# Places for raw float64 weights, the order of the first weight fetches, and a new written order in a float32 attention + gated-layer kernel

## The chip, the core and the metric

The kernel runs on one core of a Trainium2 chip. TensorE (PE in the profile; PEld is its weight load), VectorE (DVE), ScalarE (ACT), GpSimd (POOL) and SyncE (SP, which here issues every DMA) run side by side, each through its own instructions in program order, and wait for one another on semaphores. The metric is the device time of one launch in microseconds (us), less is better.

## What is computed

Band attention for 8 batches of 8 heads (512 local rows of width 64, window 32, and 32 global rows per batch), followed by a gated layer over all 8 x 544 = 4352 rows of width 512:

```python
out_g = sm(scale * q_g @ [k_g, k_l]^T) @ [v_g, v_l]
out_l = sm([scale * q_l @ k_g^T, banded scale * q_l @ k_l^T]) @ [v_g, v_l]
x = rows of [out_g, out_l], heads side by side         # 4352 x 512
a = x @ w1;  b = x @ w2                                # 512 x 1024 each
h = (a * b) @ w3                                       # 1024 x 1024
out = h @ w_out                                        # 1024 x 512
```

q, k and v are float32. The four weight matrices arrive as float64 (20 MB), so the kernel fetches their 64-bit words raw and makes float32 of them on the chip.

## The kernel before

**Stages.** The weights go through three stages. A *fetch* (`fetch`, L621) brings 512 raw 64-bit words per partition (512 KB) or, for the pieces called `w12s`, 256 words (256 KB). An *unpack* is a shift on DVE (step 0, L593), a scaled activation on ACT (step 2, L595) and a merge on DVE (step 3, L597). For w1 and w2 (together `w12`, eight column blocks m of 128, a hi and a lo tile each) two steps more split the float32 into hi (step 4, `hi_of`, L356) and lo (step 5, `lo_of`, L359, on DVE or POOL). w3 and w_out are not split: their product W34 = w3 @ w_out is formed first, in 64 matmuls `fold(t, j)` (L675): row block t of w3, inner block j; eight j make one t in a PSUM bank, and `fold_split` makes hi (`w34h`) and lo (`w34l`) of it.

The attention takes 32 pairs of heads m in turn: load k, q and v (`k2`, `q2`, `v`), spread the keys (`kx`), scores on PE (`sp`, L377), a masked minimum for each of 8 tiles on DVE (`mmax`), exponentials on ACT, normalize, transposes and moves, the values on PE (`av`, L431 to L442). A batch's global rows have `sg` (L473), `mg`, `eg`, `ng`, `tg`, and go through DRAM (`tgo`, `tgi`). `xh` and `xl` split the result into the hi and lo of x. The gated layer takes 17 blocks k of rows; per quarter of the columns it has `first(k, m, c)` (12 matmuls, L539 to L541; `begin` is its first 9 where the fourth pair comes late), a gate on ACT, DVE and POOL (`ga`, `gb`, `gh`, `gl`), and `second(k, m)` (6 matmuls, L571 to L573).

**Order.** Nothing is scheduled when the program is built: `PLAN` (L72 to L201) is a written list, in which "478S" says that step 478 runs on SP; the number counts the calls of `add`. `list_schedule` reads it out and only asserts that a step's dependencies stand before it. So each engine's instruction order is fixed by that list. `COST`, `RATE` and the due times served to make the list and have no part in the run.

**Where raw words lie.** A fetched piece needs a place until its last reader is through. Pieces of 512 KB use a ring of four: three buffers `raw` in a pool `early` and the tile of the global values of odd batches (`VG1`), which is not used yet (`RAW`, L66). From the fifth fetch on, each waits for the steps on the piece four before it. The pool `early` (with w_out's float32 and two w3 tiles `w3f`) is closed before the tiles of m = 4 to 7 are opened in the same memory (`open_early`, `close_early`, L602 to L614). This is why w1 and w2 come in two forms: m = 0 to 3 as 8 pieces of 512 KB through the ring (`w12`), m = 4 to 7 as 16 pieces of 256 KB through the three output buffers `o` (`w12s`, `MA = 4`).

**Order of the fetches.** `ORDER` (L61) takes w3 by t: half a row block (j = 0 to 3, or 4 to 7) per piece, and w_out by j. The first eight fetches in it are w3(0,0), wo 0, w3(1,0), wo 1, w3(2,0), wo 2, w3(3,0), wo 3; a fold (t, j) needs the half of t that holds j, and wo j.

**Idle products.** `IDLE` (L49) puts 11 matmuls of 256 columns on zeros (`idle_products`, L312) ahead of everything on PE.

Of the kernel before, what the change touches and what calls it, by code (L numbers as in the profile page):

```python
# [69 lines left out]
W3F = ("w3f", "w3f", "g", "as", "gh", "gl")  # L70

PLAN = """  # L72
    478S 0V 6S 10S 18S 12A 1V 19D 7D 480D 11D 8A 9D 2593V 481A 479S 20A 13D 520S 14S 246P 521S 16A 15D 21D 17D 522A
    482P 247P 22S 26S 34S 30S 24A 523A 23D 25D 256P 562S 27D 491D 524P 2V 28A 533D 535D 327S 257P 483D 29D 32A 38S 604S
    525D 248P 266P 485D 493D 267P 31D 35D 495D 487D 33D 489D 36A 276P 42S 537D 564A 40A 37D 539D 268P 494A 538A 527D
    529D 497D 39D 531D 488A 41D 43D 530A 46S 536A 50S 44A 277P 54S 606A 342P 343D 45D 258P 249P 3V 58S 349D 48A 47D 49D
    532A 344A 345D 51D 446S 55D 250P 52A 53D 496A 259P 56A 346D 486A 57D 59D 62S 260P 278P 484A 66S 534A 347S 269P 251P
    492A 70S 270P 261P 498A 271P 350A 60A 279P 63D 61D 490A 150S 5V 272P 64A 326S 351D 540A 68A 526A 65D 499D 352D 71D
    74S 280P 72A 281P 67D 73D 500D 69D 252P 501D 262P 502D 353S 78S 282P 273P 253P 76A 283P 348S 82S 274A 508A 275D
    509V 156S 528A 79D 565V 284D 607A 507D 80A 286P 504A 75D 285D 541D 84A 287P 354S 288P 86S 254D 505V 503V 77D 506A  # L80
    83D 263P 289P 290P 85D 563S 510A 81D 542D 255D 87D 511P 543D 296P 88A 566P 297P 152A 544D 89D 547D 151D 90S 575D
    577D 512A 94S 567D 548V 91D 579D 550A 513A 158A 92A 569D 581D 153D 157D 98S 102S 264A 571D 95D 291P 292P 546A 93D
    578A 570A 306P 549V 447S 298P 514D 293P 96A 568A 580A 97D 551A 582A 545S 573D 99D 552A 265D 515V 574A 108S 299P
    605S 576A 307P 114S 100A 159D 308P 103D 572A 101D 316P 104A 294A 553P 583D 110A 300P 105D 120S 608P 584D 301P 109D
    106A 111D 518A 516A 585D 107V 302P 303P 112A 113V 295D 116A 586D 617D 115D 162S 618A 609D 126S 117D 132S 317P 646S
    588S 587A 554A 121D 519V 619D 122A 118A 591S 611D 555A 309P 621D 123D 310P 318P 119D 590V 620A 623D 556D 613D 517V
    622A 124A 624A 125D 127D 128A 163D 593S 304A 129D 133D 558A 311P 614A 559V 134A 138S 610A 130A 305D 615D 135D 164A
    136A 319P 312P 131D 616A 320P 612A 144S 165D 589S 592S 321P 322P 140A 313P 448S 329S 137D 560A 594A 139D 625D 141D
    146A 323P 142A 687S 314A 145D 626D 147D 648A 595P 324A 647S 148A 315D 596A 143V 325D 649D 149D 557V 449S 597A 598D
    154A 600A 155D 160A 650P 601D 628D 4V 728S 627D 1803P 730A 769S 166A 161V 167V 630D 602A 1805P 659D 636A 632V 651D  # L90
    1807P 633A 631A 634A 661D 635D 168S 170A 629D 688S 169D 662A 637P 663D 171D 653D 561D 665D 1809P 172A 174S 180S
    731A 638A 173D 639A 655D 328S 657D 175D 186S 729S 599V 176A 640D 182A 642A 177D 178A 355P 181D 183D 643D 184A 1804P
    664A 1806P 179D 185V 1808P 188A 356D 1811A 187D 1810P 1817P 450S 192S 189D 190A 362D 357A 641V 191V 1812D 358D 198S
    1813A 359D 363A 1818P 1814V 193D 364D 1819P 1815P 1816P 689A 194A 204S 1821A 360S 200A 660A 195D 199D 196A 810S
    451S 201D 644A 666A 1820P 202A 197D 206A 658A 365D 603V 203D 1827P 210S 205D 652A 366S 207D 654A 208V 656A 667D
    209V 1822D 1828P 668D 1823A 669D 670D 1824V 1829P 211D 212A 1830P 1831A 216S 213D 217D 1825P 218A 673A 214A 215D
    219D 361S 220A 222S 1826P 1832D 674A 221D 690D 671A 678A 676D 367S 228S 234S 677A 223D 1837P 224A 225D 672V 1839P
    675D 226A 691P 227D 230A 1833V 1834V 229D 231D 232A 236A 240S 235D 242A 233D 237D 241D 238A 700D 243D 701A 1835P
    244A 239V 692D 1836P 702D 694D 704D 703A 705A 245D 706D 645V 696D 695A 698D 1838P 693A 699A 707A 697A 679D 708D
# [983 lines left out]
```

## Time and profile before

| | us |
|---|---|
| median of 3 runs | 761.32 (760.6 to 761.7) |
| the profiled execution, all of it | 760.83 |
| its span, first to last instruction | 759.1 |
| PE busy | 744.2 (98%) |
| DVE busy | 444.0 (58%) |
| ACT busy | 326.1 (43%) |
| POOL busy | 77.4 (10%) |

The granted clock of TensorE is 0.996 over the span; 1.00 is 2.4 GHz, 0.50 is 1.2 GHz. A row of a timeline is: start, duration, engine, line, operation, output<-input, count, and in brackets the idle time before it and what ended it. A fold shows as two matmul records. Records of one engine overlap: the next starts before the one before it has ended.

### The profile page before, as it was taken

The page shows a single profiled execution, that of the slowest core. Times are in us where ns is not written, and L with a number is a line of the kernel's source. Part 1 is how long each engine was busy: PE and PEld are TensorE (multiplying, and loading weights), DVE is VectorE, ACT ScalarE, POOL GpSimd, SP SyncE. Part 2 cuts the span into 40 slices and gives each one's busy share as a digit, 9 for nine tenths or more (in the row PEclk, how much of TensorE's full clock was granted, in tenths as well). Part 3 has the DMA queues.
Part 4 walks back from the last instruction along what each step waited for, and adds up shares of the span by engine and source line. Part 5 has one row for each costly group of instructions (what it writes and reads, how often), then busy time and mean ns, then how long its engine had stood idle before and what let it go on. Part 6 is the DMA issues. An engine that isn't in the chain of part 4 may idle for free.

```text
span 759.1 us, 22082 instructions
## 1 busy us (share of the span) xinstructions
PE 744.2 (98%) x9228; PEld 652.0 (86%) x9228; DVE 444.0 (58%) x1351; ACT 326.1 (43%) x1000; POOL 77.4 (10%) x145
## 2 busy tenths in 40 slices
PE   7999799999999999999999999999999999999998
PEld 5344588989999999889998999889989999999997
DVE  3889987685665655483558465755567464412121
ACT  3757875543643343353445234444444343312111
POOL 2012331322000000000001011000001010000000
PEclk9999999999999999999999999999999999999999
DMA  8897675025312311241113311331113010000000
GB/s 282 306 279 247 212 205 162 17 73 147 119 60 70 115 46 31 75 136 57 48 39 103 114 49 46 94 117 32 59 33 118 16 44 6 32 1 29 1 28 28
DMA packets 44411, 69.72 MB, mean 92 GB/s; under 512 B 8120, under 2 KB 18584, under 8 KB 44312
## 3 DMA queue, kind: packets, MB, share of 16 engines
q1 hardware_dynamic: 44312, 68.32, 28.8%
q8 instruction: 72, 1.18, 0.6%
q14 instruction: 27, 0.22, 0.1%
HBM read 53.74 MB, written 13.37 MB: 88 GB/s over the span
## 4 chain that ended last, share of the span: by engine, by line
PE 83%; DVE 2%; ACT 1%; DMA 1%; issue 0%; POOL 0%; SPq 0%; DVEq 0%; ACTq 0%; POOLq 0%
PE bp L539 8%; PE ap L539 8%; PE acc L571 8%; PE acc L573 8%; PE acc L572 8%; PE ap L540 8%; PE bp L541 8%; PE bp L540 8%; PE ap L541 8%; PE s L377 4%; PE av L431 3%; PE av L440 2%; PE av L436 2%; PE sg L473 1%; DMA raw_w12s<-in_w_t_dram 1%; ACT P L388 0%
## 5 line engine op out<-in xcount | busy, mean ns | idle before, releaser
L539 PE MATMUL ap<-x,w12h 128*128 128x256 f32 x544 | 153.0, 281 | 0.7 <-ACT as__1656 L545 0.7
L539 PE MATMUL bp<-x,w12h 128*128 128x256 f32 x544 | 152.8, 281 | 0.0
L540 PE MATMUL ap<-x,w12h 128*128 128x256 f32 x544 | 151.1, 278 | 0.5 <-DVE x L359 0.5
L541 PE MATMUL ap<-x,w12l 128*128 128x256 f32 x544 | 151.0, 278 | 0.0
L541 PE MATMUL bp<-x,w12l 128*128 128x256 f32 x544 | 150.7, 277 | 0.0
L540 PE MATMUL bp<-x,w12h 128*128 128x256 f32 x544 | 150.7, 277 | 0.0
L388 ACT ACTIVATE P<-P,small 128x128 f32<-128x128 f32 x256 | 101.0, 396 | 28.5 <-DVE small L382 28.0
L539 PEld LDWEIGHTS ap<-x,w12h 128*128 128x128 f32 x544 | 102.5, 188 | 4.6 <-issue 1.8
L539 PEld LDWEIGHTS bp<-x,w12h 128*128 128x128 f32 x544 | 102.1, 188 | 5.0 <-issue 3.0
L382 DVE CUSTOM_DVE_ANT_0 P<-s,cs 128x128 f32<-128x128 f32 x256 | 64.7, 285 | 68.0 <-PE s L377 68.0
L540 PEld LDWEIGHTS ap<-x,w12h 128*128 128x128 f32 x544 | 102.6, 189 | 2.1 <-DVE x L359 0.7
L540 PEld LDWEIGHTS bp<-x,w12h 128*128 128x128 f32 x544 | 102.3, 188 | 1.6
L541 PEld LDWEIGHTS ap<-x,w12l 128*128 128x128 f32 x544 | 102.6, 189 | 0.0
L541 PEld LDWEIGHTS bp<-x,w12l 128*128 128x128 f32 x544 | 102.3, 188 | 0.0
L675 PE MATMUL w<-wo,w3f 128*128 128x512 f32 x128 | 58.6, 607 | 4.9 <-DVE wo L597 4.9
L420 ACT COPY PT<-TT 32x256 f32<-32x256 f32 (+1 forms) x98 | 38.0, 387 | 36.1 <-DVE TT L403 18.5
L675 PEld LDWEIGHTS w<-wo,w3f 128*128 128x128 f32 x128 | 23.6, 192 | 34.8 <-issue 22.9
L356 ACT COPY u<-av 128x512 f32<-128x512 f32 (+1 forms) x58 | 22.6, 399 | 63.5 <-PE av L442 61.6
L388 ACT ACTIVATION_READ_ACCUMULATOR P<-P,small 128x1 f32 x256 | 48.2, 188 | 0.0
L377 PE MATMUL s<-KT,qp 64*32 64x128 f32 x2048 | 38.6, 283 | 2.4 <-ACT w12h L356 2.4
L403 DVE STREAM_TRANSPOSE TT<-P 128x1024 f32<-128x1024 f32 x32 | 39.6, 1237 | 0.6
L398 DVE TENSOR_TENSOR P<-P,sums 128x1024 f32<-128x1024 f32 x32 | 39.2, 1225 | 0.6
(766 smaller groups left out, 1303.9 us busy)
## 6 DMA issues: line engine op xcount, KB each, us to landing
raw_w<-in_w_t_dram SPq DMA_DIRECT2D x24, 512.0 KB, 5.3
kq<-in_kp_t_dram SPq DMA_DIRECT2D x32, 272.0 KB, 3.9
out_dram<-o_None SPq DMA_DIRECT2D x33, 256.0 KB, 2.3
qp<-in_q_t_dram SPq DMA_DIRECT2D x32, 256.0 KB, 3.0
vr<-in_v_t_dram SPq DMA_DIRECT2D x32, 256.0 KB, 3.1
gg<-tgs SPq DMA_DIRECT2D x16, 272.0 KB, 2.2
raw_wo<-in_wo_t_dram SPq DMA_DIRECT2D x8, 512.0 KB, 5.8
raw_w12s<-in_w_t_dram SPq DMA_DIRECT2D x16, 256.0 KB, 3.9
```

The costliest lines, as they stand in the source:

```text
L377: nc.tensor.matmul(st[32 * a : 32 * a + 32, x, 128 * e : 128 * e + 128], q[r, 128 * e + 32 * a : 128 * e + 32 * a + 32], k[r, o : o + 128] ...
L382: nc.vector.tensor_tensor_reduce(Ps[m % 2][:, x, e], T["s", m][:, x, 128 * e : 128 * e + 128], masks[e], -0.125, 3.0e38, ALU.add, ALU.min, ...
L388: nc.scalar.activation(p, p, AF.Exp, bias=T["mn", n][:, e : e + 1], scale=-1.0, accum_out=T["sm", m][:, x, e : e + 1])
L398: eng.tensor_mul(p, p, view(T.pop(("sm", m)), 0, [1, 8], [0, 128]))
L403: nc.vector.transpose(view(TT[:], 0, [32, 8], [256, 4], [1, 32]), view(P, 0, [128, 8], [32, 4], [1, 32]))
L539: nc.tensor.matmul(d, wh[:, k, c, :], x[:, 0, 0:w], start=(k == m % 2 == 0), stop=False, skip_group_check=True)
L540: nc.tensor.matmul(d, wh[:, k, c, :], x[:, 1, 0:w], start=False, stop=False, skip_group_check=True)
L541: nc.tensor.matmul(d, wl[:, k, c, :], x[:, 0, 0:w], start=False, stop=(k == 3), skip_group_check=True)
L571: nc.tensor.matmul(a, gh[:, m % 2, sl], wh[:, c], start=(m == 0), stop=False, **part)
L572: nc.tensor.matmul(a, gh[:, m % 2, sl], wl[:, c], start=False, stop=False, **part)
L573: nc.tensor.matmul(a, gl[:, m % 2, sl], wh[:, c], start=False, stop=(m in (5, 7)), **part)
L675: nc.tensor.matmul(T["w34", t], T["w3f", t, j // 4][:, j % 4], T["wo"][:, j], start=(j == 0), stop=(j == 7))
```

## The change

1. **Places.** The pool `early` is gone. The hi and lo tiles of w1 and w2 (16 places of 4 KB per partition: h0, l0, ... h7, l7) exist from the start, and a place holds something else until its weight is made: h4, l4, h5, l5 hold w_out in float32; l7 holds two w3 tiles; raw words lie in h6, l6, h7, `VG1` and h0 to l3, twelve places. The first 24 pieces go round these twelve, eight more (m = 0 to 3) round the first four, and m = 4 to 6 through h6, l6, h7 and l7.
2. **Larger pieces.** w1 and w2 of m = 0 to 6 come as 14 pieces of 512 KB; only m = 7 comes as 4 pieces of 256 KB.
3. **w3 by rows.** The first half of w3 (t = 0 to 3) is fetched by j: piece `w3j` j holds block j of four t, so it and wo j give four folds. In DRAM that is four runs of 1 KB per partition instead of one of 4 KB. t = 4 to 7 come as before.
4. **Order.** A new list `PLAN`: PE's order differs only in its first 151 entries of 557; from entry 152 (`second(2, 2)`, 198.6 us into the span before) to the end it is as before, and the last 1623 entries of the whole list are the same on every engine. Deciphered, PE begins with sp(0), sp(1), fold(2,0), (0,0), (1,0), (2,1), (0,1), (3,0), (1,1), (3,1), sg(0), the four folds of j = 2, of 3, of 4 and so on; before it began fold(0,0), sp(0), fold(0,1), (1,0), sp(1), (1,1), (0,2), (2,0). SP begins k2 0, wo 0, w3j 0, q2 0, k2 1, q2 1, w3j 1, wo 1, k2 2, wo 2, w3j 2, k2 3, qg 0, w3j 3, wo 3, and so on by j to wo 6; then `tgo(0)`, w3j 6, w3j 7, wo 7, `tgo(1)`; before it began k2 0, w3(0,0), wo 0, wo 1, q2 0, k2 1, w3(1,0), q2 1, w3(2,0).
5. **Idle products.** 13 instead of 11.

The diff, cut (the lists of `PLAN` are left out):

```diff
-IDLE = {None: ((0, 128, 256),) * 11}
+IDLE = {None: ((0, 128, 256),) * 13}
...
 ORDER = (
-    *[(k, a, 0) for a in range(4) for k in ("w3", "wo")], *[(k, a, e) for a in range(4) for k, a, e in (("w3", a, 1), ("wo", a + 4, 0))],
-    *[("w3", t, e) for t in range(4, 8) for e in range(2)], *[("w12", m, e) for m in range(MA) for e in range(2)],
+    *[(k, j, 0) for j in range(8) for k in ("w3j", "wo")],
+    *[("w3", t, e) for t in range(4, 8) for e in range(2)], *[("w12", m, e) for m in range(7) for e in range(2)],
 )
-RAW = ((0, "raw", 3), (0, "raw", 3), (0, "raw", 3), (1, "VG1", 1))
+RAW = ("h6", "l6", "h7", "v", *[f"{x}{m}" for m in range(MA) for x in "hl"])
+RAW = (*[RAW[n % 12] for n in range(24)], *[RAW[n % 4] for n in range(8)], "h6", "l6", "h7", "h6", "h7", "l7")
-W3F = ("w3f", "w3f", "g", "as", "gh", "gl")
+W3F = ("70", "71", "g", "as", "gh", "gl")
...
+    def at_place(name, shape, dtype, what):
+        return weights.tile(shape, dtype, tag=name, name=what)
+    def wo_of(j):
+        x = ("h4", "l4", "h5", "l5")[j // 2]
+        if ("wo", x) not in T:
+            T["wo", x] = at_place(x, [128, 2, 512], F32, f"wo{j // 2}")
+        return T["wo", x][:, j % 2]
+    def w12_of(m):
+        if m not in W12:
+            W12[m] = tuple(at_place(f"{e}{m}", [128, 4, 2, 128], F32R, f"w12{e}{m}") for e in "hl")
+        return W12[m]
...
-        nc.sync.dma_start(raw.rearrange("p a w -> p (a w)"), i(src))
+        if kind == "w3j":
+            nc.sync.dma_start(raw.rearrange("p (a b) w -> p a (b w)", a=4), i(w3_t[0:4, :, a].rearrange("a p b -> p a b")))
+        else:
+            nc.sync.dma_start(raw.rearrange("p a w -> p (a w)"), i(src))
...
+    def w3_of(t, j):
+        return ("w3j", j, 0) if t < 4 else ("w3", t, j // 4)
...
-        nc.tensor.matmul(T["w34", t], T["w3f", t, j // 4][:, j % 4], T["wo"][:, j], start=(j == 0), stop=(j == 7))
+        nc.tensor.matmul(T["w34", t], w3f_of(t, j), wo_of(j), start=(j == 0), stop=(j == 7))
...
     def made(m):
-        if m < MA:
+        if m < 7:
             return [("unit", "w12", m, e, 5) for e in range(2)]
...
-            free = [*[("w34l", j) for j in range(8)], *[("unit", *x, 5) for x in ORDER if x[0] == "w12"]] if small else []
+            free = [("fold", y, 4 * (a - 4) + z) for y in range(8) for z in range(4)] if a in (4, 5) else []
+            for x in "hl":
+                free += [z for y in rings.get(f"raw{x}{a}", ())[-1:] for z in tiles[y]]
...
-    SMALL = [("w12s", m, e) for m in range(MA, 8) for e in range(4)]
+    SMALL = [("w12s", 7, e) for e in range(4)]
```

## Rows read from the trace of the kernel before

**Rows 1.** The page: busy time of each engine, and GB/s in 40 slices.
```profile
PE 744.2 (98%) x9228; PEld 652.0 (86%) x9228; DVE 444.0 (58%) x1351; ACT 326.1 (43%) x1000; POOL 77.4 (10%) x145
...
GB/s 282 306 279 247 212 205 162 17 73 147 119 60 70 115 46 31 75 136 57 48 39 103 114 49 46 94 117 32 59 33 118 16 44 6 32 1 29 1 28 28
```
**Rows 2.** Waits of PE: who waited for whom; us in total, times, longest.
```profile
PE w L675 <- DVE wo L597: 4.9, 3, 3.3
PE s L377 <- ACT w12h L356: 2.4, 1, 2.4
PE av L431 <- DVE raw_w L593: 1.4, 1, 1.4
```
**Rows 3.** Timeline of PE, the first 75 us.
```profile
1.19 7.28 PE L318 MATMUL idle<-TT 128*128 128x256 f32 x22 [1.19 <-DVE TT L316]
11.73 1.22 PE L675 MATMUL w<-wo,w3f 128*128 128x512 f32 x2 [3.26 <-DVE wo L597]
...
17.29 1.16 PE L377 MATMUL s<-KT,qp 64*32 64x128 f32 x64
...
26.31 16.12 PE L675 MATMUL w<-wo,w3f 128*128 128x512 f32 x36
```
**Rows 4.** Stretches: length, busy of PE, PEld, DVE, ACT, POOL, clock, DMA share, GB/s.
```profile
0.00:5.00 5.00, 3.81 (x9) 3.09 (x10) 0.27 (x1) 1.28 (x1) 4.07 (x21) 1.00 0.57 168
5.00:10.00 5.00, 3.47 (x14) 2.62 (x13) 0.96 (x3) 2.28 (x5) 1.32 (x4) 1.00 1.01 361
10.00:15.00 5.00, 3.27 (x67) 2.04 (x68) 3.28 (x7) 1.21 (x2) 0.00 (x0) 0.76 0.80 265
15.00:20.00 5.00, 4.62 (x71) 2.08 (x72) 3.25 (x15) 1.88 (x4) 0.00 (x0) 0.90 0.99 360
...
50.00:60.00 10.00, 10.00 (x164) 5.49 (x163) 9.80 (x31) 6.97 (x19) 1.33 (x3) 1.00 0.86 280
...
80.00:90.00 10.00, 6.17 (x155) 4.42 (x154) 9.83 (x20) 7.94 (x20) 3.55 (x4) 0.89 0.54 186
90.00:100.00 10.00, 9.52 (x164) 8.43 (x163) 8.92 (x38) 8.04 (x24) 2.54 (x6) 0.94 0.72 211
```
**Rows 5.** Timeline of SP's DMA issues, the first 40 us.
```profile
4.48 0.61 SPq L323 DMA_DIRECT2D qp<-in_q_t_dram  x1
11.10 0.33 SPq L638 DMA_DIRECT2D raw_w<-in_w_t_dram  x1
```
**Rows 6.** Waits of SP's queue.
```profile
SPq L638 <- DVE w3f L597: 15.6, 9, 5.0
```
**Rows 7.** Timeline of DVE, 8 to 60 us.
```profile
15.48 0.43 DVE L593 TENSOR_SCALAR raw_w<-raw_w 128x512 int32<-128x512 int32 x1 [2.20 <-DMA raw_w<-in_w_t_dram]
...
35.29 0.43 DVE L593 TENSOR_SCALAR raw_w<-raw_w 128x512 int32<-128x512 int32 x1 [1.46 <-DMA raw_w<-in_w_t_dram]
```
**Rows 8.** Groups by line: count, busy us, mean ns, idle before; unpack and split on DVE.
```profile
L593 DVE TENSOR_SCALAR raw_w<-raw_w 128x512 int32<-128x512 int32 x24 | 12.7, 528 | 4.8 <-DMA raw_w<-in_w_t_dram 4.7
...
L597 DVE SCALAR_TENSOR_TENSOR raw_w12s<-raw_w12s 128x256 int32<-128x256 int32 x16 | 7.8, 489 | 1.0 <-ACT raw_w12s L595 0.3
...
L597 DVE SCALAR_TENSOR_TENSOR raw_w<-raw_w 128x512 int32<-128x512 int32 x8 | 6.6, 827 | 0.1
...
L593 DVE TENSOR_SCALAR raw_w12s<-raw_w12s 128x256 int32<-128x256 int32 x16 | 5.4, 340 | 2.0 <-DMA raw_w12s<-in_w_t_dram 1.9
L682 DVE TENSOR_TENSOR w34l<-w,w34h 128x512 fp32r<-128x512 f32 x8 | 5.4, 679 | 0.1
...
L359 DVE TENSOR_TENSOR w12l<-raw_w,w12h 128x512 fp32r<-128x512 f32 x5 | 3.4, 678 | 0.0
```
**Rows 9.** Stretches chosen for their DMAs; columns as in rows 4.
```profile
9.00:11.00 2.00, 0.00 (x0) 0.00 (x0) 1.97 (x6) 0.73 (x2) 0.00 (x0) 1.00 1.03 414
246.00:254.00 8.00, 8.00 (x112) 7.23 (x93) 6.71 (x28) 4.98 (x21) 0.87 (x2) 1.00 0.50 126
...
181.50:186.00 4.50, 4.50 (x156) 3.96 (x156) 0.72 (x6) 0.00 (x0) 0.00 (x0) 1.00 0.83 267
```

More of the change, by code (lines that the diff above doesn't have):

```diff
@@ L201 @@
+    2550P 2554S 2555A 2556S
 """.split()
@@ L637, in fetch @@
             src = w12_t[a, :, 2 * e : 2 * e + 2].rearrange("p a b c -> p (a b c)")
-        nc.sync.dma_start(raw.rearrange("p a w -> p (a w)"), i(src))
+        if kind == "w3j":
+            nc.sync.dma_start(raw.rearrange("p (a b) w -> p a (b w)", a=4), i(w3_t[0:4, :, a].rearrange("a p b -> p a b")))
+        else:
+            nc.sync.dma_start(raw.rearrange("p a w -> p (a w)"), i(src))
         T[kind, a, e] = raw
@@ L646, in unit @@
             if step > 3:
-                hi, lo = (w[:, n * e : n * e + n].rearrange("p a b c -> p (a b c)") for w in W12[a])
+                hi, lo = (w[:, n * e : n * e + n].rearrange("p a b c -> p (a b c)") for w in w12_of(a))
             if step < 4:
@@ L682, in fold_split @@
             nc.vector.tensor_sub(W34[t][1], T.pop(("w34", t)), f(W34[t][0]))
+    weights = ctx.enter_context(tc.tile_pool(name="w12", bufs=1))
     steps, after, emit, rings, tiles, late, held = [], {}, [], {}, {}, [], {}
@@ L937, in weight @@
         me = [("unit", *u, j) for j in range(6)]
-        tag = "o" if small else "raw" if ORDER.index(u) % 4 < 3 else "rawv"
-        take(tag, dict(o=NO, raw=3, rawv=1)[tag], ("raw", *u), ("fetch", *u))
+        at = "o" if small else "raw" + RAW[ORDER.index(u)]
+        take(at, NO if small else 1, ("raw", *u), ("fetch", *u))
+        if at == "rawl7":
+            late.append((("fetch", *u), [("fold", *x) for x in sorted({(t, j) for t in range(8) for j in range(8) if w3f_at(*w3_of(t, j))[0] == "7"})]))
         add(("fetch", *u), dma(390), t - 12.0, (), fetch, *u, nbytes=(262144 if small else 524288))
@@ L946, in weight @@
         read(me[3], ("raw", *u))
-        if kind == "w3":
-            tag = W3F[[x[1:] for x in ORDER if x[0] == "w3"].index((a, e)) % len(W3F)]
-            take(tag, W3F.count(tag), ("w3f", a, e), me[3])
+        if kind[:2] == "w3":
+            take(w3f_at(*u), 1, (u, "f"), me[3])
         if kind[:3] == "w12":
-            free = [*[("w34l", j) for j in range(8)], *[("unit", *x, 5) for x in ORDER if x[0] == "w12"]] if small else []
+            free = [("fold", y, 4 * (a - 4) + z) for y in range(8) for z in range(4)] if a in (4, 5) else []
+            for x in "hl":
+                free += [z for y in rings.get(f"raw{x}{a}", ())[-1:] for z in tiles[y]]
             add(me[4], hi(COST["w12h"][s], 256 if s else 512), t + 1.5, [me[3], *free], unit, *u, 4, eng=True)
@@ L958, in product @@
         due = {u: W0 + WD * n for n, u in enumerate(ORDER)}
-        due = [max(due["w3", t, j // 4], due["wo", j, 0]) + FD for j in range(8)]
+        due = [max(due[w3_of(t, j)], due["wo", j, 0]) + FD for j in range(8)]
         take(BANKS[t], 2 if BANKS[t] == "acc" else 1, ("w34", t), ("fold", t, 0))
         for j in range(8):
-            deps = [("unit", "w3", t, j // 4, 3), ("unit", "wo", j, 0, 3)] + [("fold", t, j - 1)] * (j > 0)
+            deps = [("unit", *w3_of(t, j), 3), ("unit", "wo", j, 0, 3)] + [("fold", t, j - 1)] * (j > 0)
             add(("fold", t, j), only("PE", COST["fold"]), due[j], deps, fold, t, j)
-            read(("fold", t, j), ("w34", t), ("w3f", t, j // 4))
+            read(("fold", t, j), ("w34", t), (w3_of(t, j), "f"))
         add(("w34h", t), hi_psum(COST["w34h"], 683), due[7] + 2, [("fold", t, 7)], fold_split, t, 0, eng=True)
@@ L1015, in band_attention_glu_kernel @@
             k = steps[n][0]
-            if k[0] == "unit" and k[1] == "w12s" and k[4] == 4 and "w12b" not in P:
-                close_early()
             if eng:
```

307 lines of the change are left out of this document (147 added, 160 removed).

## Prediction

> **What bounds the kernel now.** The page comes first: PE is busy for 744.2 of 759.1 us [rows 1]. Work on the other engines is worth something only where PE waits for it, so no change that leaves PE's work alone can gain more than the 14.9 us in which PE is idle and what it loses at the lower clock. The waits of PE say where the idle time lies: 4.9 us for float32 weights ahead of folds, 2.4 us ahead of a score product, 1.4 us ahead of a value product [rows 2]. That is 8.7 us; 1.2 us pass before the first idle product [rows 3], and the rest, some 5 us, is small waits and the end of the program, which the change does not touch. The timeline places the first wait: the idle products end at 8.47 us, and PE stands for 3.26 us until the first fold at 11.73 [rows 3]; two more waits ahead of folds make up the other 1.6 of the 4.9. The other two rows lie between 80 and 90 us, where PE is busy for 6.17 of 10 us [rows 4].
>
> The granted clock falls after both long waits. It averages 0.76 and 0.90 in the stretches from 10 to 20 us, and 0.89 and 0.94 from 80 to 100 us [rows 4]. With two levels, 1.2 and 2.4 GHz, 5 x 0.24 + 5 x 0.10 = 1.7 us are lost in the first place and 10 x 0.11 + 10 x 0.06 = 1.7 us in the second, less what of it fell into idle time.
>
> Why do the inputs come late? SP issues its eighth load at 4.48 us and its next at 11.10 [rows 5]: the ring of four is full, and over the run its fetches wait 15.6 us for w3 merges alone [rows 6]. DVE in turn stands idle for raw words that were asked for late (2.20, 1.46 us) [rows 7], and this backlog is worked off only by a DVE that is full from 50 to 90 us (9.80 and 9.83 of 10 in the first and last of four stretches) [rows 4]. So the 3.8 us of waits near 85 us are DVE's queue being behind, and it is behind because fetches were gated.
>
> **Places and order of fetches.** With twelve places the first twelve pieces are issued without any wait, and up to the 24th each needs only the piece twelve before it. This takes the gate off, not the bandwidth. What the front needs, up to the last fold of t = 0 to 3: 16 pieces of 0.524 MB, four `k2` of 0.279, two `q2` of 0.262, `qg` 0.066 and one `tgo` of 0.279, in all 10.4 MB. Before, the DMAs moved 282 GB/s in the first 19 us and 306 in the next 19 [rows 1]: 5.35 MB, then 5.05 / 0.306 = 16.5 us, so 10.4 MB by 35.5 us even with the gate.
>
> When does PE want it? The front of the new order is sp 0, sp 1, 32 folds and sg 0. A fold is 16.12 / 18 = 0.90 us and an sp 1.16 [rows 3], an sg about the same. The four folds of j = 7 come after 28 folds, two sp and one sg: 25.1 + 3.5 = 28.6 us of PE work. From a start at 9.4 (below) that is 38.0; two unpacks on DVE ahead of it, 2 x (0.53 + 0.68 us) for a shift and a merge (the merge taken as long as the w34l row, another DVE pass over 512 float32) [rows 8], put the last landing at 35.6. So supply and demand meet with nothing to spare: I count 0 to 4 us of new waits here and take 1.
>
> **w3 by rows.** The same 512 KB in runs of 1 KB. This form is not in the trace. The nearest rows: loads in runs of 4 KB, 414 GB/s at a share of 1.03, so 402 at full share; runs of about 2 KB, 267 / 0.83 = 322; a mix with runs of 512 bytes, 126 / 0.50 = 252 [rows 9]. Eight pieces are 4.19 MB: 10.4, 13.0 or 16.6 us. The price is 0 to 6.2 us of DMA time, I take 3, by the nearer 2 KB. Against it stands the gap that vanishes: DMAs ran at 0.57 and 0.80 of their share in 0 to 5 and 10 to 15 us [rows 4], and the second, one us at full share, is now filled. On the end of the front that leaves the 1 us already taken, with the bound widened to 5.
>
> The Trainium skill speaks against this part: "DMA: Bandwidth & Descriptors", section "Why small descriptors are slow (HBM only)", gives a fixed cost of about three cycles per packet beside one per 32 bytes. By that a run of 1 KB costs 35 / 32 against 131 / 128 for 4 KB, an estimate of 7% or 0.7 us over the eight pieces, and the sum would be some 0.5 us better than with the value I took. The mixed rows above fall off more steeply than that.
>
> **Fold order.** A pair of pieces gives four folds instead of 1, 1, 2, 2 and so on. PE starts on sp 0, which needs only k, q and two key copies; the second pair was asked for in the first microseconds. The waits ahead of folds go: gain 4.9, and 1.7 of clock. What is late next: the first fold needs the DVE steps of w3j 0 and wo 0, and one minimum of pair 0 stands between them, so DVE cannot pass before sp 0 has ended. From sp 0's end to wo 0's merge: that minimum (128 columns, taken as no longer than a shift of 512), a shift and a merge, 0.53 + 0.53 + 0.68 = 1.7 us [rows 8] against 1.16 of sp 1 [rows 3], a new gap of 0 to 0.6; I take 0.5.
>
> **DVE's queue.** Counting the list: ahead of sp 4, which ended the 2.4 us wait, DVE has 142 steps before and 120 after. The main differences are 4 large shifts, 5 large w12 merges, 3 lo's, 3 small shifts, 3 small merges and 4 w34l fewer: 4 x 0.53 + 5 x 0.83 + 3 x 0.68 + 3 x 0.34 + 3 x 0.49 + 4 x 0.68 = 13.5 us by [rows 8], some 12 as records overlap by up to 0.08 us. PE has the same work ahead of it but one fold. Ahead of the first `begin` DVE has 11 steps fewer, ahead of the first complete `first` 18. So DVE, which was 2 to 3 us too late, gets about 12 us of room at sp 4 and 5 to 7 behind it, of which PE's earlier arrival (some 6 us) takes half or more. The waits of 2.4 and 1.4 us and the second 1.7 us of clock go. Bound: 0 to 2 us of smaller waits may come in their place; none taken beyond those above.
>
> Larger pieces: 12 small pieces become 6 large ones, on DVE 12 x (0.34 + 0.49) against 6 x (0.53 + 0.83): 1.8 us less, of no worth by itself, and inside the count above.
>
> **Idle products.** Two more of 256 columns, at half a fold of 512: 2 x 0.45 = 0.9 us on PE, on the path, since sp 0 stands behind them. Its inputs, the first four loads, are 1.59 MB; 168 GB/s to 5 us and 361 after it [rows 4] gives 7.1 us and about a us to be seen. So they end at 9.4, sp 0 can run from about 8.5, and 0.9 us is the full price; if the loads came later it would be nothing.
>
> **After 200 us** nothing moves: the list is the same on every engine. A lead gained in front is kept to the end.
>
> **Sum**, against the profiled execution (759.1 of span, 1.7 around it): 4.9 + 3.8 + 1.7 + 1.7 = 12.1 off; 0.9 + 1.0 + 0.5 = 2.4 on: 9.7 us less, 751.1 for that execution. The median of the runs shown stands 0.5 above it: 751.6. With no new waits 750; with the bounds of supply (5) and of smaller waits (2) in full, less the 1.5 taken, 757.
>
> **Rivals.**
> *The front is bound by supply.* Runs of 1 KB at the mixed rate cost 6.2 us, and waits of that length drop the clock again (1.7 us as before): 751.6 + 4 + 1.7 = 757.3. For it: DMA share is at 0.99 and 1.01 in two of the first four stretches [rows 4]. Against it: the last small fetches of the front were issued late because of the gate.
> *The places do not come free as counted*, so the change does not do what it says: SP still stands ahead of fetches, since a fetch into h0 to l3 or the split of w12 into them waits for a reader far down the list, or `tgo(0)` in SP's queue holds w3j 6, w3j 7 and wo 7 up. Then the waits near 85 us stay, with their clock: 751.6 + 3.8 + 1.7 = 757.1. Against it: `tgo(0)` waits for `tg(0)`, which stands ahead of wo 4 in DVE's queue.
> *Slower.* The place is w3j; the mechanism is a cost per packet and not per byte. If a packet of 1 KB took as long as one of 4 KB, the eight pieces would take 4 x 10.4 = 41.6 us of the DMAs, 31 more, and every fold of t = 0 to 3 would wait for them: 751.6 + 31 - 1 - the 6 or so us that the rest catches up, near 775. It decides from 10 us of lost supply on, that is from 4.19 MB in over 20 us, under 205 GB/s. The row with 512-byte runs still has 252 at full share, which speaks against it.
>
> **How the numbers follow.** Forecast (749.5 to 755) 0.67; better than that 0.05; supply 0.12; places 0.10; slower 0.06. The predicted time is 751.6, the range 749 to 758, which leaves out the slower case and the far ends. About 0.2% (1.5 us) is what a measurement of this kernel can tell from no change. Faster by more: all but the slower case and a little of the supply and places cases, 0.90; within it 0.04; slower 0.06.
>
> **What would show it.** SP issues a fetch at least every two us up to 25 us, with no pause as from 4.48 to 11.10. sp 0 starts at 9.4, folds by 12, and the 32nd fold ends near 42 to 44. The clock stays at 1.00 from 10 to 20 and from 80 to 100 us. PE waits for nothing over 1.5 us, and `second(2, 2)` starts near 189 instead of 198.6. DVE is no longer full from 50 to 90 us. I am wrong if PE has waits over 2 us before 45 us that end on a merge of w3j 5 to 7 (supply), or on score products near 80 us (places).

## The result and the profile after

The changed kernel takes 753.3 us (median of four executions, 753.15 to 755.88) beside 760.96 for the kernel before on the same chip: a ratio of 0.9905, 95% interval 0.9888 to 0.9922, so 7.2 us less by the ratio. Run again beside other kernels (below) the ratio was 0.992 (0.990 to 0.9941). The forecast was 751.6, 9.7 us less than the median that was known then (761.32). The direction held, and the waits that were to go are gone. A quarter to somewhat over a third of the gain is missing, and the reason that the prediction leaned on most, the gate on the fetches, turns out to be the smaller part. The profiled execution is the longest of its four: 754.1 us of span and 1.8 around it, 5.0 us of span less than before.

The waits of PE, to be read against [rows 2]: who waited for whom, us in total, times, the longest.

```profile
PE av L431 <- ACT PT L420: 1.6, 3, 0.8
PE w L684 <- DVE w3f L597: 1.2, 2, 1.1
...
```

None of the three rows of before is left. In their place stand eleven short waits in the first 113 us, none over 1.1 us. Their places are in the timeline of PE (the rows with idle time in brackets, and sp(0) with sp(1)):

```profile
1.18 7.90 PE L318 MATMUL idle<-TT 128*128 128x256 f32 x26 [1.18 <-DVE TT L316]
9.01 2.35 PE L377 MATMUL s<-KT,qp 64*32 64x128 f32 x128
11.86 7.48 PE L684 MATMUL w<-wo,w3f 128*128 128x512 f32 x16 [0.49 <-DVE wo L597]
...
21.27 14.17 PE L684 MATMUL w<-wo,w3jf 128*128 128x512 f32 x32 [0.84 <-DVE w3jf L597]
...
49.96 1.15 PE L377 MATMUL s<-KT,qp 64*32 64x128 f32 x64 [0.54 <-DMA qp<-in_q_t_dram]
...
57.53 1.98 PE L684 MATMUL w<-wo,w3f 128*128 128x512 f32 x4 [1.08 <-DVE w3f L597]
59.69 1.12 PE L684 MATMUL w<-wo,w3f 128*128 128x512 f32 x2 [0.17 <-DVE w3f L597]
...
82.99 0.38 PE L431 MATMUL av<-PT,vr 64*64 64x96 f32 x2 [0.41 <-ACT PT L420]
...
83.77 0.96 PE L431 MATMUL av<-PT,vr 64*64 64x128 f32 x27 [0.41 <-ACT PT L420]
...
89.24 0.38 PE L539 MATMUL ap<-x,w12h 128*128 128x256 f32 x1 [0.25 <-ACT x L356]
90.59 0.38 PE L540 MATMUL ap<-x,w12h 128*128 128x256 f32 x1 [0.96 <-DVE x L359]
...
97.30 0.39 PE L539 MATMUL bp<-x,w12h 128*128 128x256 f32 x1 [0.20 <-DVE g__1210 L549]
...
112.11 1.11 PE L431 MATMUL av<-PT,vr 64*64 64x96 f32 x30 [0.82 <-ACT PT L420]
```

The idle products are followed at once by sp(0) and sp(1), and from the first fold at 11.86 to 47 us PE has one wait of 0.84 us. The stretches, columns as in [rows 4]:

```profile
10.00:15.00 5.00, 4.39 (x83) 2.17 (x72) 4.17 (x14) 1.56 (x3) 1.68 (x4) 1.00 1.05 387
15.00:20.00 5.00, 5.00 (x26) 1.77 (x25) 3.67 (x27) 3.41 (x11) 0.97 (x2) 1.00 1.08 377
...
60.00:70.00 10.00, 10.00 (x165) 5.63 (x164) 9.90 (x27) 9.57 (x23) 5.47 (x6) 1.00 0.84 316
...
80.00:90.00 10.00, 8.56 (x201) 6.11 (x201) 9.76 (x29) 8.60 (x21) 3.79 (x3) 1.00 0.54 186
90.00:100.00 10.00, 9.21 (x76) 9.01 (x77) 9.62 (x26) 8.70 (x26) 4.54 (x5) 1.00 0.61 195
```

The granted clock is 1.00 where it was 0.76, 0.90, 0.89 and 0.94 [rows 4]. DVE, however, is as full as it was. What the lead is worth is seen at `second(2, 2)`, from which on the order is the same in both kernels; it started at 198.6 us before. This row groups the products of one source line and tile (minimum, median and maximum in ns, first and last start):

```profile
L571 PE MATMUL acc<-w34h,gh__2632 x4: 388/388/390, 192.7 to 194.8; 128*128 128x512 f32 x4
```

So the lead is 5.9 us there, where 9.6 were forecast. It can be added up. All that was to go has gone: 4.9 + 3.8 + 1.7 + 1.7 = 12.1. With it went two small waits which the forecast had left standing, 0.48 us near 99 us and 0.74 at 129. The timeline of PE in the kernel before shows the second of them, and the score product sp(4) with the old wait of 2.4 us:

```profile
87.71 1.96 PE L377 MATMUL s<-KT,qp 64*32 64x128 f32 x64 [2.42 <-ACT w12h L356]
...
129.20 0.38 PE L539 MATMUL ap<-x,w12h 128*128 128x256 f32 x1 [0.74 <-ACT as__1656 L545]
```

Gone are 13.3 us, then. Come instead: the idle products 0.6 (7.90 beside 7.28 us [rows 3]), the gap ahead of the first fold 0.5, and new waits of 0.84 + 0.54 + 1.08 + 0.17 + 0.41 + 0.41 + 0.25 + 0.96 + 0.20 + 0.82 = 5.7. That is 13.3 - 6.8 = 6.5, beside the 5.9 measured. The clock explains part of the difference: the prediction took it at 1.7 us for each of the two places in full, although some of it fell into idle time. The forecast had 1.0 us for the new waits in place of 5.7. The experiments ask three things: which part of the change made the old waits go, what the parts that cost something cost, and what the new waits come from.

### The profile page after: what moved, and what is told of

It reads as the page before. It is cut to its first block, busy times and chain, and to the rows that moved or that the text cites. A ratio compares the mean times of both kernels' runs of the same rounds, so it can differ in the third digit from the quotient of the medians.

```text
span 754.1 us, 22008 instructions
## 1 busy us (share of the span) xinstructions
PE 742.1 (98%) x9232; PEld 650.6 (86%) x9232; DVE 438.8 (58%) x1332; ACT 326.6 (43%) x989; POOL 84.3 (11%) x153
## 4 chain that ended last, share of the span: by engine, by line
PE 81%; DVE 7%; DMA 5%; ACT 3%; issue 1%; SPq 1%; DVEq 0%; ACTq 0%
PE bp L539 8%; PE ap L539 8%; PE acc L573 8%; PE acc L571 8%; PE acc L572 8%; PE ap L540 8%; PE ap L541 8%; PE bp L540 8%; PE bp L541 8%; PE s L377 4%; PE av L431 4%; DMA raw_w<-in_w_t_dram 3%; PE av L440 2%; PE av L436 2%; DMA raw_wo<-in_wo_t_dram 1%
## 5 line engine op out<-in xcount | busy, mean ns | idle before, releaser
L684 PE MATMUL w<-wo,w3f 128*128 128x512 f32 x96 | 43.4, 600 | 1.8 <-DVE w3f L597 1.2
L431 PEld LDWEIGHTS av<-PT,vr 64*64 64x64 f32 x1024 | 28.1, 132 | 13.0 <-issue 8.4
L462 POOL TENSOR_TENSOR xg<-u 128x32 f32<-128x32 f32 x32 | 8.7, 272 | 267.7 <-ACT u L356 233.4
```

The costliest lines, as they stand in the source:

```text
L431: nc.tensor.matmul(av[c, y, 128 * k + 32 * s0 : 128 * k + 32 * s1], V[r, x, k], PT[r, s0:s1, x, k], start=(k == 0), stop=False, **go)
L684: nc.tensor.matmul(T["w34", t], w3f_of(t, j), wo_of(j), start=(j == 0), stop=(j == 7))
```

## Experiments

All but the first were timed in five rounds, and all beside the kernel before on the same chip. The chips differ by some 0.2%, so the ratio to the kernel before is what compares.

| kernel | median us | ratio to before | 95% |
|---|---|---|---|
| changed, first time | 753.3 | 0.9905 | 0.9888 to 0.9922 |
| changed, again | 755.64 | 0.992 | 0.990 to 0.9941 |
| four places, by rows | 758.06 | 0.9936 | 0.9915 to 0.9957 |
| twelve places, by t | 760.95 | 0.9993 | 0.998 to 1.0007 |
| four places, by t | 763.94 | 1.0031 | 1.0012 to 1.0051 |
| before with 13 idle products | 761.8 | 0.9998 | 0.9984 to 1.0012 |
| changed with 11 idle products | 753.63 | 0.9888 | 0.9864 to 0.9912 |
| changed, w3 in whole runs | 755.13 | 0.9907 | 0.9887 to 0.9927 |
| changed, SP's order | 752.95 | 0.9873 | 0.9852 to 0.9894 |
| changed, GpSimd apart | 754.4 | 0.9904 | 0.9884 to 0.9925 |
| all moves together | 750.38 | 0.985 | 0.983 to 0.9871 |
| the same, w3 in whole runs | 749.03 | 0.983 | 0.9811 to 0.9849 |
| the same, runs of 1 KB, DVE's order | 749.18 | 0.9831 | 0.981 to 0.9852 |

The changed kernel again, as the yardstick of the second batch:

> The changed kernel once more, beside the next three on the same chip. It sets what they are compared with. Expected: ratio 0.990 to 0.992 to the kernel before, as in its first measurement, with the same new waits ahead of folds, of the first value products of pair 3 and near 90 us.

It came out at 0.992 with the same new waits (1.05 us ahead of a fold near 57 us, 0.69 for a load of q, 0.97 near 90 us). Below, 0.9912 stands for the changed kernel, the mean of its two ratios.

### Which part took the old waits away

**Four places.** The order on each engine is that of the changed kernel; only eight of the first 16 pieces lie elsewhere.

```diff
-RAW = (*[RAW[n % 12] for n in range(24)], ...
+RAW = (*[RAW[n % (4 if n < 16 else 12)] for n in range(24)], ...
```

> The changed kernel with four places, not twelve, for the first 16 pieces of weights (the eight by rows of w3 and the eight of w_out); the order of the instructions on every engine is as it was. My theory: it was the ring of four that made the inputs of the folds late. SP again stands for several us after its eighth load or so, the folds of the first 45 us wait for 4 us or more in all, the granted clock falls below 1.00 after the longest of these waits, and the program is 4 to 8 us longer than the changed kernel: 757 to 761. Rival (the gain comes from the order by rows alone, which asks for less before the first four folds, and the places matter little): 753 to 755, with SP's pauses hidden behind folds.

SP's issues show the gate again, as in [rows 5]: it stands from 5.9 to 12.8 and from 16.2 to 23.0 us.

```profile
5.05 0.86 SPq L329 DMA_DIRECT2D kq<-in_kp_t_dram  x1
12.79 0.33 SPq L637 DMA_DIRECT2D raw_wo<-in_wo_t_dram  x1
...
15.91 0.33 SPq L637 DMA_DIRECT2D raw_wo<-in_wo_t_dram  x1
22.95 0.38 SPq L635 DMA_DIRECT2D raw_w3j<-in_w_t_dram  x1
```

Yet PE hardly felt it. Its waits for folds of this kernel:

```profile
PE w L684 <- DVE w3f L597: 2.9, 3, 1.7
...
PE w L684 <- DVE wo L597: 1.1, 2, 0.8
...
PE w L684 <- DVE w3jf L597: 0.8, 1, 0.8
```

That is 4.8 us beside 2.5 in the changed kernel, the granted clock stays at 1.00, and the time is 0.9936 against 0.9912: 1.8 us, with intervals that overlap, where my theory said 4 to 8. Neither theory as written holds in full. The gate is real, but by rows most of its wait falls beside folds that are there to be done.

**By t.** Twelve places, but the first half of w3 by t, and the 32 folds in the order of the kernel before, in the slots where the folds of t = 0 to 3 stood. (Two DVE steps of w3(3,0) had to stand ahead of a minimum of the global scores, or the order would have locked.)

```diff
 ORDER = (
-    *[(k, j, 0) for j in range(8) for k in ("w3j", "wo")],
+    *[(k, a, 0) for a in range(4) for k in ("w3", "wo")], *[(k, a, e) for a in range(4) for k, a, e in (("w3", a, 1), ("wo", a + 4, 0))],
...
-        return ("w3j", j, 0) if t < 4 else ("w3", t, j // 4)
+        return ("w3", t, j // 4)
```

> The changed kernel with twelve places as it is, but the first half of w3 fetched by t again, half a t in each piece, and the 32 folds of t = 0 to 3 in the order in which the kernel before had them, in the places of the list where the folds stood. My theory: both parts were needed for the front. By t the folds that a new pair of pieces allows are 1, 1, 2, 2 and not four, so PE runs out of folds before 20 us although the fetches are early: waits ahead of folds of 2 to 5 us in all before 40 us, and the program is 2 to 6 us longer than the changed kernel. Rival: the early fetches are all that matters; then the time stays within 1 us of the changed kernel's and the fetch by rows has no worth of its own.

The time is that of the kernel before, 6.2 us above the changed kernel by the ratios, just past the end of what I had expected. PE's timeline, two of its seven waits ahead of folds before 40 us, and the stretch from 10 to 15 us:

```profile
15.64 2.84 PE L684 MATMUL w<-wo,w3f 128*128 128x512 f32 x6 [1.80 <-DVE wo L597]
...
32.39 5.55 PE L684 MATMUL w<-wo,w3f 128*128 128x512 f32 x12 [2.24 <-DVE wo L597]
...
10.00:15.00 5.00, 3.34 (x130) 1.97 (x130) 4.34 (x16) 1.64 (x3) 1.50 (x4) 1.00 1.04 416
```

In all PE waits 8.3 us for w_out and w3 here, with every fetch issued early. By t, k pieces allow about k x k / 4 folds (1, 4, 9, 16 after 2, 4, 6, 8 pieces); by rows 2 k (4, 8, 12, 16). PE runs dry between pieces although the DMAs move over 400 GB/s from 10 to 20 us.

**Neither.** Both edits at once.

> Both parts of the front undone in the changed kernel: four places for the first 16 pieces, and the first half of w3 by t with the folds in the order of the kernel before. It fills the fourth corner beside twelve places by rows (the changed kernel), four places by rows (0.9936 of the kernel before) and twelve places by t (0.9993). My theory now: by t the folds are short of pairs even when every fetch is early, so the gate adds little there, 0 to 2 us: 761 to 763, about the kernel before, and what the rest of the change gains near 85 us is given back by a list that was not made for this front. Rival: places and rows are separate gains that add up; then it is 2 to 3 us slower than twelve places by t, 763 to 764, a ratio of 1.002 to 1.004.

The rival came true: 1.0031, 2.9 us above twelve places by t. So the two parts nearly add up: by rows instead of by t is worth 6.2 us with twelve places and 7.2 with four; twelve places instead of four 1.8 us by rows and 2.9 by t. The waits ahead of folds do not show what the places are worth by t: they add up to 8.3 us in the kernel with neither, too. In the profiled executions the clock differs. After a wait of 2.2 us near 32 us, twelve records of folds took 7.11 us in the kernel with neither and 5.55 (above) by t with twelve places. The stretch from 35 to 40 us (the clock is the third number from the right) has 0.80 with neither and 1.00 by t with twelve places:

```profile
32.96 7.11 PE L684 MATMUL w<-wo,w3f 128*128 128x512 f32 x12 [2.23 <-DVE wo L597]
...
35.00:40.00 5.00, 5.00 (x10) 1.92 (x8) 4.02 (x12) 2.03 (x5) 0.00 (x0) 0.80 0.97 365
```

```profile
35.00:40.00 5.00, 3.70 (x9) 1.44 (x8) 4.80 (x11) 3.07 (x8) 0.00 (x0) 1.00 0.72 270
```

These are single executions. Over all of them, the mean clock of the span is 0.993 to 0.998 with neither and 0.995 to 0.999 by t with twelve places (0.996 or less in eight of twelve), and 0.999 or 1.000 by rows, with four places as with twelve. So the clock tells rows from t and not twelve places from four; what makes up the 2.9 us is not settled.

One limit: the rest of the list was made for rows. By t in a list made for it need not be as bad: the kernel before, by t with four places in its own list, waits for folds for only 4.9 us [rows 2], where the kernel with neither waits for 8.3. So the 6 to 7 us are the price of t in this list. Another limit: the runs with four places give them to the first 16 pieces only.

### What the parts that cost something cost

**Idle products.** First the kernel before with 13 of them, `IDLE` alone changed.

> The kernel before with 13 idle products instead of 11; nothing else. It tells whether the two products have a part in the granted clock's staying up. My theory: PE still waits for the first merge, so the products end inside that wait and cost nothing; the wait gets about 0.6 us shorter, the granted clock still falls below 1.00 between 10 and 20 us, and the time is the same within 0.5 us. Rival: the shorter wait no longer takes the clock down; then it is 1.00 from 10 to 20 us and the program is 1 to 2 us shorter, and up to 1.7 us of the change's gain belong to the idle products and not to the fetches.

The time is the same (0.9998). The wait ahead of the first fold is 2.76 instead of 3.26 us, and the granted clock falls all the same (10 to 15 us, the column before the DMA share):

```profile
12.05 1.61 PE L675 MATMUL w<-wo,w3f 128*128 128x512 f32 x2 [2.76 <-DVE wo L597]
...
10.00:15.00 5.00, 2.95 (x58) 1.71 (x66) 3.58 (x8) 1.46 (x3) 0.00 (x0) 0.76 0.74 252
```

So the two products alone do not keep the clock up. Then the changed kernel with 11.

> The changed kernel with 11 idle products ahead of the first score product instead of 13; nothing else differs. My theory: the two products lie in time in which the inputs of the first score product are already there, so leaving them out lets it start about 0.6 us earlier (0.62 us is what the two cost by the two profiles, 0.9 us is what I had taken), and the program is 0.3 to 0.9 us shorter, near 752.7, with the granted clock still at 1.00 after 10 us. Rival: the first score product then waits for its loads, and the time is the same within 0.3 us. Second rival: the clock is held up by these two products; then it falls below 1.00 between 10 and 20 us and the program is 1 to 2 us longer.

The ratio is 0.9888 against 0.9912, 1.8 us better, with intervals that overlap. The clock stays at 1.00, so the second rival is out. That would be more than the products' own time. In the profiled execution the waits of 0.54, 1.08 and 0.17 us between 49 and 60 us are missing, too. Whether that follows from the earlier start is not settled: sp(0) started at 8.07 us here and at 8.44 in the second profile of the changed kernel, which had them. SP, however, was through the second group of loads of `tgi` (below) at 42.6 us here, and at 45.4 and 44.1 in the two profiles of the changed kernel.

**Runs of 1 KB.** A second copy of the half of w3 in DRAM, by rows in whole runs.

```diff
-            nc.sync.dma_start(raw.rearrange("p (a b) w -> p a (b w)", a=4), i(w3_t[0:4, :, a].rearrange("a p b -> p a b")))
+            nc.sync.dma_start(raw.rearrange("p a w -> p (a w)"), i(w3j_t[:, a]))
```

> The changed kernel, with a second copy of the first half of w3 in memory, laid out so that each piece by rows lies in whole runs of 4 KB instead of runs of 1 KB. Everything else is as it was. My theory in the prediction took 3 us of DMA time and 1 us of the end for the short runs. After the look at the changed kernel's profile, where the DMAs moved 370 to 400 GB/s at a full share while these pieces arrived, I expect no difference: 753.3 within 0.5 us, and the idle stretch of the DMAs near 25 us only begins up to 1 us earlier. Rival (the front is bound by supply, because of the short runs): the time falls by 1 us or more, and the waits ahead of folds before 60 us get shorter by as much.

No difference beyond the intervals: 0.9907. The DMAs do see one. Packets and the queue's share of 10 to 20 us, first of the changed kernel (again), then of this one:

```profile
DMA packets 2437, 3.81 MB, mean 381 GB/s; under 512 B 143, under 2 KB 1785, under 8 KB 2436
...
q1 hardware_dynamic: 2436, 3.79, 105.9%
```

```profile
DMA packets 1384, 4.11 MB, mean 411 GB/s; under 512 B 151, under 2 KB 279, under 8 KB 1383
...
q1 hardware_dynamic: 1383, 4.10, 102.7%
```

Whole runs go at 4.11 MB / 10.27 us = 400 GB/s at full share. In the first, some 1640 packets of 1 KB are 1.68 MB; the other 2.13 MB at 400 take 5.3 of the 10.6 us, which leaves 5.3 for the 1.68 MB: about 320 GB/s. By this estimate the eight pieces cost 13.1 instead of 10.5 us of the DMAs, 2.6 us. The profile of whole runs shows where these go: the DMAs are nearly idle at 24 to 28 us, in all for some 2 us more than in the changed kernel.

```profile
24.00:26.00 2.00, 1.90 (x5) 0.57 (x3) 1.72 (x4) 2.00 (x8) 0.00 (x0) 1.00 0.15 59
26.00:28.00 2.00, 1.94 (x5) 0.98 (x6) 1.93 (x8) 2.00 (x10) 0.00 (x0) 1.00 0.03 8
```

### What the new waits come from

**SP's order.** In the changed kernel the DMAs run dry while SP stands. The rows show its issues, and then two stretches:

```profile
16.19 1.15 SPq L637 DMA_DIRECT2D raw_wo<-in_wo_t_dram  x2
26.70 0.33 SPq L504 DMA_DIRECT2D gg<-tgs  x1
27.08 1.15 SPq L635 DMA_DIRECT2D raw_w3j<-in_w_t_dram  x2
...
40.38 4.50 SPq L510 DMA_DIRECT2D TGr<-gg  x4
```

```profile
26.00:28.00 2.00, 2.00 (x7) 0.79 (x5) 2.00 (x5) 2.00 (x7) 0.00 (x0) 1.00 0.25 85
...
42.00:44.00 2.00, 2.00 (x6) 0.90 (x5) 1.21 (x5) 1.98 (x8) 0.00 (x0) 1.00 0.38 80
```

`tgo(0)` (L504) holds SP for 9 us with three fetches behind it; `tgi` (L510) and its waits do the same near 40 us. The edit lets fetches pass.

```diff
+for w, x in (
+    ("54S", "311S"), ("62S", "311S"), ("66S", "311S"),   # w3j 6, w3j 7, wo 7 ahead of tgo(0)
+    ("70S", "317S"), ("78S", "317S"), ("74S", "317S"),   # three of w3 ahead of tgo(1)
+    ("86S", "318S"), ("102S", "318S"), ("527S", "290S"), # w3, w12 ahead of tgi(1); q2 2 ahead of vg
+):
+    PLAN.remove(w)
+    PLAN.insert(PLAN.index(x), w)
```

> The changed kernel with nine entries of SP's list moved: the last two pieces of w3 by rows and the last of w_out ahead of the first store of the summary scores (which waits for DVE), three pieces of w3 ahead of the second, two pieces ahead of its loads, and one load of q ahead of the loads of the values. My theory: the waits that are new in the changed kernel at 50 to 60 us (0.5 + 1.1 + 0.2 us) come from SP's queue, where fetches stand behind an instruction that waits, while the DMAs run dry from 24.5 to 27.5 and from 42 to 48 us. They then go, and the program is 1 to 1.8 us shorter, near 752. Rival: DVE's queue sets these waits and the fetches were early enough; then nothing changes within 0.4 us. Second rival: the fetches now delay the second half of the summary scores, whose reader, the first value product near 48 us, waits up to 3 us, and the program is 1 to 3 us longer.

0.9873, 3.0 us better, more than expected. The waits of 0.54, 1.08 and 0.17 us are gone, and the DMA share is 1.12 in both stretches above. Nothing but SP's list was touched, so letting fetches pass a waiting SP is enough to take them away. They come to 1.8 us; the rest of the 3.0 is within the intervals. That the run with 11 products lacked them too, with SP's list as it was, fits SP's being through with `tgi` earlier there, but was not tested by itself.

**GpSimd beside VectorE.** In that run a shift on DVE took 1.60 us and delayed a fold by 1.05; near 87 us a step `xl` took 1.31. POOL's rows of the same kernel say what it did then (DVE first, then POOL):

```profile
13.81 1.60 DVE L600 TENSOR_SCALAR raw_wo<-raw_wo 128x512 int32<-128x512 int32 x1
...
87.21 1.31 DVE L366 TENSOR_TENSOR x<-u,x 128x256 fp32r<-128x256 f32 x1 [0.21 <-ACT x L363]
```

```profile
13.29 0.95 POOL L314 MEMSET VG<- 128x1024 f32 x1
14.18 0.96 POOL L307 MEMSET PT<- 128x1024 f32 x1
...
86.95 1.29 POOL L366 TENSOR_TENSOR w12l<-raw_w,w12h 128x512 fp32r<-128x512 f32 x1 [1.63 <-ACT w12h L363]
```

The shift ends at 15.41, 0.27 us behind the end of the second clear; without company it takes 0.43. The merge ahead of it, from 13.21 us on, kept its usual 0.69 us beside the first clear. The moves for these two steps in a kernel of their own:

```diff
+    ("3V", "487V"), ("2V", "487V"),   # POOL clears VG and PT ahead of its copy for kx(1, 1)
+    ("154A", "137V"),                 # ACT: hi of w12(4, 0) behind xh(0, 3, 0)
```

> The changed kernel with three entries of the list moved: GpSimd clears the two tiles for values and probabilities at 5 to 8 us, ahead of its copy of the second keys, and not at 13 to 16 us; and ScalarE makes the high part of a piece of w1 and w2 behind, not ahead of, the high part of the last heads' outputs near 86 to 90 us. My theory: steps of VectorE take 1.3 to 1.6 us instead of 0.43 and 0.69 where GpSimd works at the same time, and this is what makes the wait of 0.96 us ahead of a gate product near 90 us, and, in runs where the first score product comes late, a wait of 1.0 to 1.3 us ahead of a fold near 15 us. Both waits then go, and the program is 1.0 to 2 us shorter than the changed kernel. Rival: VectorE's queue is merely full there; the steps keep their length, the waits move by no more than 0.3 us, and the time is the same within 0.4 us.

`xl` takes 0.41 us again (the row below), and the waits of 0.25 and 0.96 us near 90 us are gone; one of 0.84 for `gb` has come where 0.41 was. The shift near 14 us still took 0.86, since POOL's copy of keys remains beside it. 0.9904 against 0.992 in the same batch: 1.2 us, within the intervals, at the lower end of the theory.

```profile
87.95 0.41 DVE L366 TENSOR_TENSOR x<-u,x 128x256 fp32r<-128x256 f32 x1
```

**All together.** 11 products, both sets of moves, and three small ones for the other new waits.

```diff
-IDLE = {None: ((0, 128, 256),) * 13}
+IDLE = {None: ((0, 128, 256),) * 11}
...
+    ("11D", "447D"), ("13D", "447D"),   # wo 0: shift, merge ahead of the first minimum
+    ("456A", "28A"), ("448A", "28A"),   # two exps ahead of the scale of wo 2
...
+for w in ("593", "596"):                # two of eight moves of pair 3 on POOL
+    PLAN.remove(w + "A")
+    PLAN.insert(PLAN.index("600V") + 1, w + "V")
```

> The changed kernel with 11 idle products, the order of SP's list as in the run with nine entries moved, GpSimd's and ScalarE's three entries as in the run before this one, and three small moves more: the shift and the merge of the first piece of w_out ahead of the first minimum, two exponentials ahead of a scale that waits for its load near 14 us, and two of eight copies of pair 3 on GpSimd and not at the end of ScalarE's queue. My theory: the new waits of the changed kernel add up (0.6 us for two products, 0.5 to 0.8 ahead of the first fold, 0.8 ahead of a fold at 21 us, 0.5 to 1.8 at 50 to 60 us, 0.8 and 1.2 at 80 to 91 us), each has its own cause, and they can be had together: 3.5 to 5 us less than the changed kernel. Rival: VectorE is full from 30 to 100 us, so what is won in front comes back as waits near 80 us; then 1 to 2 us less at most.

0.985, 4.7 us less than the changed kernel by the ratios, 5.3 by the medians of this batch: as expected, and against the rival that a full DVE would give it back. DVE still shows 9.94 and 9.72 of 10 from 60 to 80 us. The longest wait left is 1.02 us ahead of a fold at 34.35, and DVE's timeline of this kernel names its cause:

```profile
31.78 0.71 DVE L514 STREAM_TRANSPOSE tgs<-Pg 128x512 f32<-128x512 f32 x1 [1.30 <-DMA gg<-tgs]
```

`tg(1)` waits until the store `tgo(0)` has landed, and with the fetches let past, the DMAs are full to 30 us. Two kernels attack this from two sides: whole runs (the edit above), and DVE's order:

```diff
+    ("316D", "464D"), ("317S", "464D"),   # tg(1) and tgo(1) behind the merge of w3j 6
```

> The best kernel so far (all moves together, 750.4 us) with the first half of w3 in whole runs of 4 KB, as in the run of that name. My theory: runs of 1 KB do cost DMA time, about 2.5 us for the eight pieces (322 GB/s by the bytes and packets of 10 to 20 us, against 400 for whole runs), and it was hidden only because SP stood still from 17 to 26 us. In the best kernel SP fetches on, the DMAs are full to 30 us, the first store of the summary scores lands only near 31.7, and VectorE waits 1.3 us for it and PE 1.0 us ahead of a fold. With whole runs the DMAs get there 2 us earlier, both waits go, and the program is 0.7 to 1.2 us shorter. Rival: the price of short runs never reaches PE; then the wait stays and the time is the same within 0.3 us.

> The best kernel so far, with the second transpose of the summary scores behind two merges in VectorE's list instead of ahead of them, and its store behind it in SP's. Runs of w3 stay at 1 KB. My theory: the same wait of VectorE (1.3 us for the first store's landing) can be taken away by giving it other work first: PE's wait of 1.0 us ahead of a fold near 34 us goes, and the program is 0.7 to 1.1 us shorter than the best so far, 749.4 beside 750.4. Rival: the second half of the summary scores then comes too late for the first value product near 46 us, PE waits there instead, and the time is the same or up to 1 us longer.

Both do it: 0.983 and 0.9831, some 1.5 us less each (the intervals overlap with that of the kernel without), and in neither does a fold wait over 0.2 us. So what the short runs cost the DMAs does reach PE once SP no longer stands still: the wait of 1.02 us goes with whole runs. Here it can be hidden again by the order alone. At 749.0 and 749.2 us these are the fastest versions, some 6 us under the changed kernel.

## Why the forecast was right, and where it was off

**What bounds the kernel, and what goes.** Right: PE's three large waits and both stretches at a lower clock are gone, 12.1 us in all by the prediction's count. That this total held does not confirm the causes behind it, since the change altered places, pieces and order at once.

**Places.** The pause of SP from 4.48 to 11.10 us is gone, as said. The step that failed is the weight it was given: "late because fetches were gated" explained nearly all of the front. Four places by rows cost 1.8 us only, with intervals that overlap.

**Fold order.** It was named as the reason that the waits ahead of folds go, in a sentence without a number. By the four corners the shape of the pieces carries 6 to 7 us in this list, the larger share. Rows of before could have told: PE's longest wait, 3.26 us [rows 3], was for the first piece of w_out, the third load of SP and behind no gate. The first fold is no earlier now (11.86 beside 11.73); two score products fill the time ahead of it. So this wait went by PE's new order, which all four corners share (0.21 us is left ahead of the first fold with neither), and not by places or rows.

**w3 by rows.** 3 us of DMA time were taken, by the row with runs of 2 KB; 2.6 come out of the packets and shares above. The Trainium skill, "DMA: Bandwidth & Descriptors", section "Why small descriptors are slow (HBM only)", gave an estimate of 0.7 us for it, by its cost per packet; the packets and shares give almost four times that. The 1 us that it was to cost at the end was nothing, because SP's stand at `tgo(0)` left the DMAs idle anyway.

**The rival of places that do not come free** was half right. `tgo(0)` did hold w3j 6, w3j 7 and wo 7 up, and "at least every two us up to 25 us" fails from 17 us on. The reason against it, that `tg(0)` stands ahead of wo 4 in DVE's queue, said nothing of when that is: 26 us. Its price was wrong too: not the old waits near 85 us, but most likely the new ones at 50 to 60.

**DVE's queue.** The waits of 2.4 and 1.4 us went as the count of its steps said. That DVE was behind "because fetches were gated" is not borne out for the first 16 pieces: with four places by rows, where SP stands as before, sp(4) starts 4.8 us earlier than in the kernel before (87.71) and waits for nothing.

```profile
82.92 1.16 PE L377 MATMUL s<-KT,qp 64*32 64x128 f32 x64
```

The later pieces keep their twelve places in that run, so their part is not told from that of the fewer steps.

That DVE would no longer be full was wrong (9.90, 9.72 and 9.76 of 10 from 60 to 90 us). A full engine with the right step in front makes no one wait. What took the old waits' place there, 0.82 for ACT's moves near 83 us, 1.41 from 89 to 98 and 0.82 at 112, I had put at nothing, with a bound of 2: this is the term most out of size, 3.0 us.

**Smaller waits in front.** 1.5 us taken (1.0 of supply and 0.5 of the gap ahead of the first fold), 3.1 measured up to 60 us (0.49 + 0.84 + 0.54 + 1.25). The gap itself was 0.49 in the first profile and 0.81 in the second.

**Idle products.** 0.9 taken as their full price, 0.85 measured in the mean of all profiles: nine with 26 records take 8.29 us (7.33 to 8.87), five with 22 records 7.44 (6.96 to 8.05). One pair of executions tells nothing, since the same products differ by more than that from one to another (below).

**After 200 us.** The lead was kept but for 0.7 us of one wait near 334 us.

## What to carry to other kernels

When inputs come late, ask what a newly landed piece allows the bottleneck to do, before asking how early it was requested: here, in a list made for rows, the shape of the pieces was worth some three times the depth of the ring. A fix of one gate shows the next one in the same queue, so read, for every instruction that waits on the DMA-issuing engine, what stands behind it. And count small waits that take the place of a large one at more than nothing.
